# Border units in quarters, wider narrow products and filler products in a two-layer decode kernel

## The chip, the core and the metric

The kernel runs on one core of a Trainium2 chip. The metric is the device time of one execution in microseconds. A profile of one execution gives a span, from the first to the last instruction, and the times of every instruction and DMA packet.

## The reference

One token for each of 4 sequences passes twice through a grouped-query attention block over a cache and a gated feed-forward block (FFN). Both layers use the same weights and the same cache.

```python
B, Sq, D = 4, 1, 512
Hq, Hkv, Sk, Dh = 32, 8, 8192, 128          # k_cache, v_cache: [B, Hkv, Sk, Dh], bf16
F = 1792                                    # w_gate, w_up: [D, F]; w_down: [F, D]

def _A_ref(x, k_cache, v_cache, wq, wo):
    q = (x @ wq) as [B, Hq, 1, Dh]
    scores = einsum("bhqd,bhkd->bhqk", q, repeat(k_cache, 4)) * Dh ** -0.5
    o = einsum("bhqk,bhkd->bhqd", softmax(scores), repeat(v_cache, 4))
    return o as [B, 1, Hq * Dh] @ wo

def _B_ref(x, w_gate, w_up, w_down):
    return (silu(x @ w_gate) * (x @ w_up)) @ w_down

x = x + _A_ref(_layernorm(x), ...); x = x + _B_ref(_layernorm(x), ...)
x = x + _A_ref(_layernorm(x), ...); x = x + _B_ref(_layernorm(x), ...)
```

## The kernel before

**Units and slots.** A unit is one pair of sequence and key-value head: 32 in a layer, each with 2 MB of K and 2 MB of V. "K0" or "V31" below is the K or V of unit 0 or 31. SBUF holds 8 slots of 2 MB (`kvf`, seen as `kv`); slot and place in it are named `s{slot}.{block}`, 8 blocks a slot. Layer 0 goes through units 0 to 31; layer 1 (`unit_order[1]`) through 29, 30, 31, which are kept in SBUF from layer 0, and then 0 to 28. The FFN weights lie in slots 6 and 7 (gate first, then a quarter of up, then down) and in some room of their own (the rest of up), which is loaded once.

**One unit.** `keys` (lines 527 to 549) turns each block of K in place on VectorE (`turn`, a stream transpose of 128x512 words) and emits, a few blocks behind (`drain`, `LAG`), the score products of a block on TensorE (`scores`: four matmuls that stream 256 columns). After the eighth block come the softmax steps (`max_p`, `max_t`, `exps`, `turn_p`, `total`) on DVE, PE and ACT, spread over the following blocks by gaps in `line`. `values` multiplies by V: two blocks of 8 matmuls of 512 columns, then `own_first`, `own_others`, `add_rows`; the last two units of a layer take `block_last` instead, 64 matmuls of 4 columns each. After the four units of a head `out_proj` adds its share of `wo` to `xT`. `work` (line 312) sets the order: K of a unit, then V of the unit before it. The blocks that K30 and K31 of layer 1 bring have no transposes, since they were turned in layer 0.

**Loads.** All loads are issued on SP's queue in the order of the list `items`. `pump` (line 373) issues the next item when its slot (`home`) is free; a slot comes free when its unit is `finished`. SP waits, in order, on the semaphore of the engine that reads the slot. A whole unit is one DMA whose source is cut into contiguous runs (`runs`); the last V of a layer (`split`) comes in four column ranges. At the start of layer 1, V0 takes the slot of K29 and K2 that of K30, in two halves each (`half`, `halves`): the first after four blocks are scored, the second after eight. K0 and K1 go to slots 6 and 7, which `ffn` frees at its end (line 731) for the waits of the single loads.

**The border.** After the last unit `center` computes the mean and the squares, `ffn` (line 699) multiplies by gate (56 tiles of 128x128, 4 columns), up (56) and down in three groups of 6, 6 and 2 of its 14 tile rows (`WD`), with the loads of down in the same groups; `add_to_x` adds each group's product. Then layer 1 begins with `center`, the query products of unit 29's head and their rows (`qproj`), and the units. The other heads' query products (112 matmuls of 4 columns) are one entry of `blocks` before K0 (line 807).

**Emission.** PE, DVE and ACT instructions are recorded on tapes (`T.pe`, `T.op`; helper lines 99 and 117 are what the profile names) and played at the end by `roll`, which puts the longest run of alike units of each layer in a loop on each engine.

Of the kernel before, what the change touches and what calls it, by code (L numbers as in the profile page):

```python
# [145 lines left out]
def bass_interleave_layers__gqa_block_cached__swiglu_ffn__decode_kernel(  # L146
# [18 lines left out]
    P = 128  # L165
# [19 lines left out]
    RUN = 1 << 15  # L185
    assert TB == 2 * NA and NV * REP <= QB
# [4 lines left out]
    with ExitStack() as es:  # L191
# [16 lines left out]
        wd_sb = kvf[:, f1:f1 + FO * D].rearrange("p (f n) -> p f n", f=FO)  # L208
        places = [f"s{s}.{q}" for s in range(NKEEP, NSLOT) for q in range(NB)]
        room = lambda a, b: places[(a - f0) // (TB * Dh):(b - 1 - f0) // (TB * Dh) + 1]  # L210
        at_w = {"wg": room(f0, f0 + KT * F) + ["wg"], "wu": room(f0 + KT * F, f1) + ["wu", "wu3"],
                "wd": room(f1, f1 + FO * D)}
        WD = ((0, 6), (6, 12), (12, 14))
# [43 lines left out]

        SBK = [0, 1]
# [8 lines left out]
        sem_h = [[sem(f"sem_h{k}{i}") for i in range(2)] for k in range(2)]  # L267
# [57 lines left out]
        for n, it in ((3, ("wo", 0)), (6, ("wo", 1)), (9, ("wo", 2)), (12, ("wo", 3))):  # L325
            items.insert(n, it)
        ends = [i for i, it in enumerate(items) if it[0] == "wd"]
        split = {items[e - 3] for e in ends}

        halves = {("K", 1, unit_order[1][k]): items[ends[0] + 3 + k] for k in range(2)}  # L330
# [42 lines left out]
        def pump():  # L373
            while issued[0] < len(items):
                n = issued[0]
                it = items[n]
                if it[0][0] == "w":
                    if it[0] == "wg":
                        if not {NKEEP, NKEEP + 1} <= free:
                            return  # L380
                        free.difference_update((NKEEP, NKEEP + 1))
                    load_weight(*it)
                    issued[0] += 1
                    continue

                s = home(it)
                if s not in free:
                    return
                free.remove(s)
                kind, L, u = it  # L390
                slot_of[it] = s
                g, b = unit_gb(u)
                cache = A_k_cache if kind == "K" else A_v_cache
                src = cache[b, g, :, :].rearrange("(p t) d -> p (t d)", p=P)
                if it in split:
                    w = TT * Dh // NQ
                    n8 = NB // NQ
                    for q in range(NQ):
                        T.dma("sp", [(kv[:, s, q * w:(q + 1) * w], src[:, q * w:(q + 1) * w])], sem_l[q],
                              writes=[f"s{s}.{q * n8 + k}" for k in range(n8)])  # L400
                else:
                    T.dma("sp", [(kv[:, s, :], runs(cache[b, g, :, :]))], sem_s[s], writes=[f"s{s}.{q}" for q in range(NB)])
                issued[0] += 1

        def half(it, i):
            to = halves[it]
            kind, L, u = to
            s = slot_of[it]
            if i == 0:
                assert items[issued[0]] == to  # L410
                slot_of[to] = s
                issued[0] += 1
            w = SL // 2
            src = (A_k_cache if kind == "K" else A_v_cache)[u % B, u // B, :, :].rearrange("(p t) d -> p (t d)", p=P)
            T.dma("sp", [(kv[:, s, i * w:(i + 1) * w], src[:, i * w:(i + 1) * w])], sem_h[unit_order[1].index(it[2])][i],
                  writes=[f"s{s}.{i * NB // 2 + k}" for k in range(NB // 2)])

        def finished(it):
# [5 lines left out]
            elif it in halves:  # L424
                half(it, 1)
                pump()
            else:
                free.add(slot_of[it])
                pump()
# [97 lines left out]
        def keys(L, u):  # L527
            def block(q):
# [9 lines left out]
                if q == NB // 2 - 1 and ("K", L, u) in halves:  # L538
                    half(("K", L, u), 0)
# [4 lines left out]

            for q in range(NB):
                if (L, u, q) not in turned:
                    turn(L, u, q)
                blocks.append((0.65, lambda q=q: block(q)))
                drain(LAG)
        done = set()  # L550
        def values(L, u):
# [36 lines left out]
            def add_rows():  # L588
                T.pe(bank(LNB)[:, 0:REP], acc[:], head[:], reads=["acc", "head"], writes=[f"pb{LNB}"],
                     start=True, stop=True)  # L590
                scale_o(LNB)

            def block_last(q):
# [6 lines left out]
                for t in range(q * TB, (q + 1) * TB):  # L600
                    c0 = (t % TB) * QB + REP * q
                    T.pe(bank(bk)[:, 0:REP], kv[:, s, t * Dh:(t + 1) * Dh], pT[:, turn_of[u], c0:c0 + REP],
# [5 lines left out]
            def scale_o(k):  # L608
                T.op("dve", lambda e: e.tensor_tensor(oT[:, g // (G - 1), :, b], bank(k)[:, 0:REP], rl[:, rl_of[u], :],
# [21 lines left out]
        def out_proj(g):  # L631
# [10 lines left out]
            for nt in range(KT):  # L642
                for c in range(REP):
                    T.pe(bank(OUTB)[:, nt * B:(nt + 1) * B], ((c, nt), wo_at(c * D + nt * P)), o4[:, c, :], at=g,
# [7 lines left out]
        def center():  # L652
            T.op("dve", lambda e: e.tensor_reduce(vs[:], xT[:].rearrange("p (k b) -> p b k", b=B), AX.X, ALU.add),
                 reads=["x"], writes=["vs"])
            T.pe(bank(LNB)[:, 0:B], ones, vs[:], start=True, stop=True,
                 reads=["vs", "onesf"], writes=[f"pb{LNB}"])
            total = bank(LNB)[:, 0:B].unsqueeze(1).to_broadcast([P, KT, B])
# [18 lines left out]
        def qproj(gs, u=None):  # L676
            h0, nh = gs[0] * REP, len(gs) * REP
            for h in range(h0, h0 + nh):
                for kt in range(KT):
                    T.pe(bank(LNB)[:, h * B:(h + 1) * B], wq_sb[:, kt, h * Dh:(h + 1) * Dh], xn[:, kt * B:(kt + 1) * B],  # L680
                         start=(kt == 0), stop=(kt == KT - 1),
                         reads=[f"wq{kt}", "xn"], writes=[f"pb{LNB}"], sig=(kt == KT - 1))
            T.op("dve", lambda e: e.tensor_copy(qT[:, :, h0:h0 + nh],
# [5 lines left out]
            for c in range(4):  # L689
                for a in range(NA):  # L690
                    T.pe(ob[a * QB:(a + 1) * QB, c, :, h0:h0 + nh], pick[:, c // 2, :, c % 2], qT[:, :, h0:h0 + nh],
                         start=True, stop=True,
                         reads=["pT1", "ident"], writes=[f"pb{OUTB}"], sig=(a == NA - 1))
            if u is not None:
# [4 lines left out]
        def ffn(last):  # L699
# [4 lines left out]
            rb = rstd[:].unsqueeze(1).to_broadcast([P, FO, B])  # L704
            for (w_sb, wname, bk) in (([wg_sb[:, k, :] for k in range(KT)], "wg", gb), (wu_sb, "wu", ub)):
                for fo in range(FO):
# [3 lines left out]
                    for kt in range(KT):  # L710
                        T.pe(bank(bk)[:, fo * B:(fo + 1) * B], w_sb[kt][:, f:f + 2 * P - 1:2], xn[:, kt * B:(kt + 1) * B],
                             start=(kt == 0), stop=(kt == KT - 1),
                             reads=at_w[wname] + ["xn"], writes=[f"pb{bk}"], sig=(fo == FO - 1 and kt == KT - 1))
            T.op("dve", lambda e: e.tensor_tensor(fb(gr), fb(gT), rb, ALU.mult),
# [8 lines left out]
            for j, (a, b) in enumerate(WD):  # L723
                for nt in range(KT):
                    for fo in range(a, b):
                        T.pe(bank(dn[j])[:, nt * B:(nt + 1) * B], wd_sb[:, fo, nt * P:(nt + 1) * P],
                             hT[:, fo * B:(fo + 1) * B], start=(fo == a), stop=(fo == b - 1),
                             reads=["hT", f"wd{j}"] + at_w["wd"], writes=[f"pb{dn[j]}"], sig=(fo == b - 1))
                if j < len(WD) - 1:
                    add_to_x(dn[j])  # L730
            free.update((NKEEP, NKEEP + 1))
            pump()
# [65 lines left out]
        for L in range(2):  # L798
            turn_of.update((u, i % 2) for i, u in enumerate(unit_order[L]))
            rl_of.update((u, i % CYCLE) for i, u in enumerate(unit_order[L]))  # L800
            center()
            first = unit_order[L][0] // B
            qproj([first], unit_order[L][0])
            rest_q = [list(range(0, first)), list(range(first + 1, G))]
            assert (L, first) in ((0, 0), (1, G - 1))
            for i, (kind, _, u) in enumerate(work(L)):
                if L == 1 and (kind, u) == ("K", 0):
                    blocks.append((3.5, lambda gs=rest_q[0]: qproj(gs)))
                (keys if kind == "K" else values)(L, u)
                if L == 0 and i == 0:  # L810
                    drain(0.0)
                    qproj(rest_q[1])
# [45 lines left out]
```

## Time and profile before

| | |
|---|---|
| runs | 650.14 us median of 3 (649.64 to 650.25) |
| profiled execution | 651.29 us, its span 649.3 us |
| mean granted TensorE clock | 0.855 |
| PE, PEld, DVE, ACT, POOL busy | 505.3, 324.7, 446.2, 116.3, 19.3 us |
| HBM read | 273.88 MB, 422 GB/s over the span |
| whole-unit loads, issue to landing | 28.8 us (K), 31.2 us (V) |
| score matmuls, 128x256 | x2048, 332.6 us busy, 305 ns mean |
| DVE transposes of K, 128x512 | x488, 322.3 us busy, 686 ns mean |

PE is TensorE's matmul row, PEld its weight loads, SPq SyncE's issue of DMAs. A line such as `ps<-kvf,zq 128*128 128x256 bf16` is a matmul into PSUM with a stationary tile of 128x128 and 256 streamed columns. Busy times of PE are of pipelined matmuls, so they overlap. Times in timelines count from the start of the span.

### The profile page before, as it was taken

The page shows a single profiled execution, that of the slowest core. Times are in us where ns is not written, and L with a number is a line of the kernel's source. Part 1 is how long each engine was busy: PE and PEld are TensorE (multiplying, and loading weights), DVE is VectorE, ACT ScalarE, POOL GpSimd, SP SyncE. Part 2 cuts the span into 40 slices and gives each one's busy share as a digit, 9 for nine tenths or more (in the row PEclk, how much of TensorE's full clock was granted, in tenths as well). Part 3 has the DMA queues.
Part 4 walks back from the last instruction along what each step waited for, and adds up shares of the span by engine and source line. Part 5 has one row for each costly group of instructions (what it writes and reads, how often), then busy time and mean ns, then how long its engine had stood idle before and what let it go on. Part 6 is the DMA issues. An engine that isn't in the chain of part 4 may idle for free.

```text
span 649.3 us, 12407 instructions
## 1 busy us (share of the span) xinstructions
PE 505.3 (78%) x4896; PEld 324.7 (50%) x4896; DVE 446.2 (69%) x1079; ACT 116.3 (18%) x391; POOL 19.3 (3%) x73
## 2 busy tenths in 40 slices
PE   1657788878868787886877986898888787886886
PEld 1534454545435454553556654555555454553556
DVE  2556676776866767776762386979797777686683
ACT  0021111211211212221220211213131221121120
POOL 0000000000000000000000000000000000000000
PEclk9998787797987879789795978979897969799795
DMA  8999999999999999999999999999999999999996
GB/s 347 427 431 428 433 429 434 428 440 428 432 436 424 444 426 432 439 424 442 428 416 361 421 408 430 417 439 430 432 438 424 438 430 436 436 424 438 430 415 279
DMA packets 13085, 274.27 MB, mean 422 GB/s; under 512 B 2712, under 2 KB 2720, under 8 KB 3744
## 3 DMA queue, kind: packets, MB, share of 16 engines
q1 hardware_dynamic: 13056, 273.89, 98.7%
q8 instruction: 17, 0.28, 0.2%
q14 instruction: 12, 0.10, 0.0%
HBM read 273.88 MB, written 0.00 MB: 422 GB/s over the span
## 4 chain that ended last, share of the span: by engine, by line
DMA 50%; DVE 24%; PE 21%; issue 3%; SPq 1%; ACT 1%; DVEq 0%; POOL 0%; ACTq 0%; POOLq 0%
DMA kvf<-in_A_k_cache_dram 47%; PE ps L99 21%; DVE kvf L117 15%; DVE acc L117 4%; DMA kvf<-in_B_w_up_dram 3%; DVE one L117 1%; DVE pT L117 1%; SPq L135 1%; DVE m L117 1%; DVE scr L117 1%; ACT pb L117 0%; ACT acc L117 0%; DVE oT L117 0%; DVEq L782 0%; SPq L133 0%
## 5 line engine op out<-in xcount | busy, mean ns | idle before, releaser
L117 DVE STREAM_TRANSPOSE kvf<-kvf 128x512 f32<-128x512 f32 x488 | 322.3, 686 | 68.6 <-DMA kvf<-in_A_k_cache_dram 68.6
L99 PE MATMUL ps<-kvf,zq 128*128 128x256 bf16 x2048 | 332.6, 305 | 21.7 <-DVE kvf L117 16.4
L99 PEld LDWEIGHTS ps<-kvf,zq 128*128 128x128 bf16 x2048 | 202.6, 111 | 92.7 <-DVE kvf L117 40.2
L117 ACT ACTIVATE pb<-m 1x128 f32<-1x128 f32 x64 | 19.7, 308 | 441.1 <-DVE m L117 441.1
L99 PE MATMUL ps<-kvf,pT 128*16 128x512 bf16 x960 | 68.0, 407 | 1.4 <-DVE rl L117 1.4
L117 DVE SCALAR_TENSOR_TENSOR acc<-ps,own,acc 128x128 f32<-128x128 f32 x180 | 63.2, 351 | 6.5 <-ACT acc L117 1.9
L99 PE MATMUL ps<-identf,one 128*1 128x128 f32 x64 | 17.9, 279 | 43.2 <-DVE one L117 43.2
L117 DVE TENSOR_REDUCE one<-ps 128x1 f32<-128x256 f32 x64 | 25.9, 405 | 37.0 <-PE ps L99 36.5
L99 PEld LDWEIGHTS ps<-identf,one 128*1 128x1 f32 x64 | 5.1, 80 | 73.6 <-DVE one L117 67.5
L99 PE MATMUL ps<-head,acc 128*128 128x4 f32 x120 | 24.5, 275 | 21.4 <-DVE acc L117 21.3
L99 PEld LDWEIGHTS ps<-head,acc 128*128 128x128 f32 x120 | 20.5, 214 | 37.0 <-DVE acc L117 36.7
L117 ACT ACTIVATE pb<-ps,one,rstd 128x256 bf16<-128x256 f32 x64 | 36.1, 563 | 2.1
L467 POOL TENSOR_TENSOR zq<-scr,quad 128x64 bf16<-128x64 bf16 x62 | 18.1, 293 | 604.0 <-PE ps L99 564.9
L99 PEld LDWEIGHTS ps<-kvf,pT 128*16 128x16 bf16 x960 | 19.1, 91 | 33.8 <-issue 21.9
L99 PE MATMUL ps<-one,pb 1*128 1x1 f32 x128 | 26.2, 272 | 11.5 <-ACT pb L117 11.2
L99 PEld LDWEIGHTS ps<-one,pb 1*128 1x128 f32 x128 | 20.8, 202 | 28.8 <-ACT pb L117 26.0
L99 PE MATMUL ps<-o,wo_sb 128*128 128x4 bf16 x256 | 26.5, 166 | 9.1 <-DVE o L117 9.1
L117 DVE STREAM_TRANSPOSE pT<-pb 128x256 bf16<-128x256 bf16 x64 | 26.1, 408 | 9.7 <-ACT pb L117 9.7
L99 PEld LDWEIGHTS ps<-rsm,one 128*128 128x128 f32 x128 | 23.9, 232 | 12.2 <-ACT rsm L117 10.4
L99 PEld LDWEIGHTS ps<-o,wo_sb 128*128 (+1 forms) x256 | 22.8, 103 | 12.8 <-issue 9.0
L99 PE MATMUL ps<-rsm,one 128*128 128x4 f32 x128 | 21.7, 240 | 9.0 <-ACT rsm L117 9.0
L117 DVE TENSOR_TENSOR xT<-xT,ps 128x16 f32<-128x16 f32 x21 | 3.6, 172 | 33.1 <-PE ps L99 33.1
(61 smaller groups left out, 197.1 us busy)
## 6 DMA issues: line engine op xcount, KB each, us to landing
kvf<-in_A_k_cache_dram SPq DMA_DIRECT2D x60, 2048.0 KB, 28.8
kvf<-in_A_v_cache_dram SPq DMA_DIRECT2D x58, 2048.0 KB, 31.2
wq_sb<-in_A_wq_dram SPq DMA_DIRECT2D x4, 1024.0 KB, 8.4
wo_sb<-in_A_wo_dram SPq DMA_DIRECT2D x8, 512.0 KB, 37.7
kvf<-in_A_v_cache_dram SPq DMA_DIRECT2D x8, 512.0 KB, 14.7
kvf<-in_B_w_gate_dram SPq DMA_DIRECT2D x8, 448.0 KB, 16.8
kvf<-in_B_w_down_dram SPq DMA_DIRECT2D x14, 256.0 KB, 17.6
kvf<-in_B_w_up_dram SPq DMA_DIRECT2D x5, 448.0 KB, 18.0
```

The lines of the kernel that those rows point to most:

```text
L99: return e.matmul(out, lhsT=lhsT if at is None else lhsT(place(at)), rhs=rhs, **kw)
L117: self.tape[engname].append((repr((name, args, kw)), lambda e, _: getattr(e, name)(*args, **kw), left, sig, None))
L135: ins = e.add_instruction(mybir.InstDMACopy(name=self.nc.get_next_instruction_name(), mode="Copy", queue="qSPDynamicHW", ins=e.lower_ap_dm ...
L467: T.op(eng, lambda e: e.tensor_tensor(dst, q4, m4_, ALU.mult), reads=keys_ + ["quad"], writes=["zq"])
```

## The change

It has four parts. (1) The units at the borders (the last of each layer, and 0, 1 and 2 of layer 1, `fours`) are laid out as four contiguous quarters of their tokens and loaded by quarters (`part`); V0 and K2 come into the slots of K29 and K30 by quarters, after every second scored block (`quarter`, `heirs`); K0 and K1 are issued inside `ffn`, piece by piece: three quarters of K0 after the gate products, the fourth after up, half of K1 after the first group of down, half after the last. The groups of down are 8, 4 and 2, and each names its own places. (2) The order at the start of layer 1: K0 and K1 are turned while K30 and K31 are scored (`ahead`); V31 comes before K0; V3 is loaded before K4; the query products of the other heads become seven entries and their rows an eighth. (3) Products of 4 columns repeat them to 32 (`few`, `WIDE`); the 28 others overwrite columns of the bank that are not yet, or no longer, in use. (4) `warm` adds products that nobody reads to the start of layer 1: two and one around the sum in `center`, one after the first query products, one after their rows. `qproj` is split into `qmul` and `qrows` for it, and `add_rows` moves to other columns of its bank.

```diff
+    WIDE = 32
...
-        WD = ((0, 6), (6, 12), (12, 14))
+        WD = ((0, 8), (8, 12), (12, 14))
...
-                "wd": room(f1, f1 + FO * D)}
+                **{f"wd{j}": room(f1 + a * D, f1 + b * D) + [f"wd{j}"] for j, (a, b) in enumerate(WD)}}
...
+        def few(ap):
+            n = ap.shape[1]
+            return ap.unsqueeze(1).to_broadcast([P, WIDE // n, n])
...
+        i, j = (items.index((k, 1, unit_order[1][2 * NRES + n])) for k, n in (("K", 1), ("V", 0)))
+        items[i], items[j] = items[j], items[i]
...
+        heirs = {("K", 1, unit_order[1][k]): items[ends[0] + 3 + k] for k in range(2)}
+        fours = {(L, unit_order[L][-1]) for L in range(2)} | {(1, u) for u in unit_order[1][NRES:2 * NRES]}
...
+        def part(it, s, a, b, sem_):
+            kind, L, u = it
+            n = NB // NQ
+            w, m = n * TB * Dh, S // NQ
+            src = (A_k_cache if kind == "K" else A_v_cache)[u % B, u // B, :, :]
+            T.dma("sp", [(kv[:, s, q * w:(q + 1) * w], runs(src[q * m:(q + 1) * m, :])) for q in range(a // n, b // n)],
+                  sem_, writes=[f"s{s}.{k}" for k in range(a, b)])
...
+        def quarter(it, i):
+            to = heirs[it]
+            if i == 0:
+                place(to, slot_of[it])
+            n = NB // NQ
+            part(to, slot_of[it], i * n, (i + 1) * n, sem_h[unit_order[1].index(it[2])][i])
...
-                if q == NB // 2 - 1 and ("K", L, u) in halves:
-                    half(("K", L, u), 0)
+                if ("K", L, u) in heirs and (q + 1) % (NB // NQ) == 0 and q < NB - 1:
+                    quarter(("K", L, u), q // (NB // NQ))
...
+            i = unit_order[L].index(u)
+            ahead = unit_order[1][i + 2] if L == 1 and i in (1, 2) else u
             for q in range(NB):
-                if (L, u, q) not in turned:
-                    turn(L, u, q)
+                if (L, ahead, q) not in turned:
+                    turn(L, ahead, q)
...
-                    T.pe(bank(bk)[:, 0:REP], kv[:, s, t * Dh:(t + 1) * Dh], pT[:, turn_of[u], c0:c0 + REP],
+                    T.pe(bank(bk)[:, 0:WIDE], kv[:, s, t * Dh:(t + 1) * Dh], few(pT[:, turn_of[u], c0:c0 + REP]),
...
+        def warm(n=1):
+            for _ in range(n):
+                T.pe(bank(SBK[1])[:, 0:SW], wq_sb[:, 0, 0:P], wq_sb[:, 0, 0:SW], reads=["wq0"], writes=[f"pb{SBK[1]}"],
+                     start=True, stop=True)
...
-        def center():
+        def center(n=0):
...
+            warm(2 * n)
             T.pe(bank(LNB)[:, 0:B], ones, vs[:], start=True, stop=True,
                  reads=["vs", "onesf"], writes=[f"pb{LNB}"])
+            warm(n)
...
+            ks = items[ends[0] + 1:ends[0] + 3]
+            w6 = KT * F // (TB * Dh) // 2 * 2
...
+                if not last:
+                    if bk == gb:
+                        place(ks[0], NKEEP)
+                        part(ks[0], NKEEP, 0, w6, sem_p[0])
+                    else:
+                        part(ks[0], NKEEP, w6, NB, sem_p[1])
...
+                if j == 0 and not last:
+                    place(ks[1], NKEEP + 1)
+                    part(ks[1], NKEEP + 1, 0, NB // 2, sem_p[2])
-            free.update((NKEEP, NKEEP + 1))
-            pump()
+            if not last:
+                part(ks[1], NKEEP + 1, NB // 2, NB, sem_p[3])
...
-            center()
+            center(L)
...
+            todo = work(L)
+            if L == 1:
+                todo.remove(("V", 1, unit_order[1][2]))
+                todo.insert(todo.index(("K", 1, 0)), ("V", 1, unit_order[1][2]))
...
-                if L == 1 and (kind, u) == ("K", 0):
-                    blocks.append((3.5, lambda gs=rest_q[0]: qproj(gs)))
+                if L == 1 and (kind, u) == ("V", unit_order[1][2]):
+                    for k in rest_q[0]:
+                        blocks.append((0.5, lambda k=k: qmul([k])))
+                    blocks.append((0.5, lambda gs=rest_q[0]: qrows(gs)))
```

## The prediction

> **What bounds the kernel.** I read the page's queue table and chain of waits first, then a table of windows, then SP's and PE's timelines around the places that the windows pointed to.
>
> ```profile
> q1 hardware_dynamic: 13056, 273.89, 98.7%
> ...
> DMA 50%; DVE 24%; PE 21%; issue 3%; SPq 1%; ACT 1%; DVEq 0%; POOL 0%; ACTq 0%; POOLq 0%
> ```
>
> The reader is to see that one queue moves 273.89 MB and is nearly always occupied, and that half of the chain is DMA. So the time is bytes over rate, plus the stretches in which the stream does not run at its rate. The windows (start:end, length, busy time and count of PE, PEld, DVE, ACT, POOL, then granted clock, DMA share, GB/s) give both:
>
> ```profile
> 100.00:300.00 200.00, 159.91 (x1294) 98.19 (x1291) 144.18 (x338) 35.91 (x122) 6.15 (x21) 0.84 1.00 433
> ...
> 325.00:345.00 20.00, 15.38 (x298) 12.10 (x299) 11.64 (x36) 4.10 (x14) 0.29 (x1) 0.83 0.99 415
> 345.00:350.00 5.00, 3.19 (x108) 2.93 (x105) 0.85 (x6) 0.00 (x0) 0.00 (x0) 0.50 0.94 303
> 350.00:355.00 5.00, 3.55 (x45) 2.82 (x46) 1.47 (x9) 0.56 (x2) 0.00 (x0) 0.50 0.75 321
> 355.00:360.00 5.00, 4.50 (x26) 2.95 (x24) 0.42 (x1) 0.00 (x0) 0.29 (x1) 0.64 0.99 421
> 360.00:380.00 20.00, 18.18 (x256) 13.37 (x257) 9.44 (x26) 5.07 (x17) 0.58 (x2) 0.89 1.04 442
> 380.00:385.00 5.00, 5.00 (x42) 3.15 (x43) 3.72 (x8) 0.00 (x0) 0.29 (x1) 0.75 0.96 377
> 385.00:390.00 5.00, 4.04 (x33) 2.65 (x31) 4.92 (x14) 1.77 (x6) 0.00 (x0) 1.00 0.92 374
> 390.00:400.00 10.00, 5.23 (x47) 3.10 (x48) 6.53 (x15) 1.77 (x6) 0.29 (x1) 0.98 0.98 419
> 400.00:420.00 20.00, 17.96 (x155) 10.85 (x155) 17.91 (x42) 4.42 (x16) 0.88 (x3) 0.92 1.01 428
> ...
> 645.00:649.30 4.30, 1.66 (x36) 1.22 (x36) 0.87 (x4) 0.00 (x0) 0.00 (x0) 0.50 0.00 1
> ```
>
> In the steady stretch the stream moves 433 GB/s. At that rate 273.89 MB take 632.5 us, so 16.8 us of the 649.3 us span are lost somewhere. A window's loss is its length times (1 - GB/s / 433). The border between the two layers loses 1.50, 1.29, 0.14, -0.42, 0.65, 0.68, 0.32 and 0.23 us from 345 to 420: together **4.4 us**. The rows for 300 to 325 and for 420 to 625 stand at 430 to 433. The last 4.3 us carry nothing. What may be won lies in these two places.
>
> SP's timeline says why the border loses:
>
> ```profile
> 347.99 2.38 SPq L135 DMA_DIRECT2D kvf<-in_A_k_cache_dram  x2
> 356.84 3.07 SPq L133 DMA_DIRECT2D kvf<-in_A_v_cache_dram  x2
> 362.13 2.85 SPq L133 DMA_DIRECT2D kvf<-in_A_k_cache_dram  x2
> 365.63 0.48 SPq L135 DMA_DIRECT2D kvf<-in_A_v_cache_dram  x1
> 370.70 0.48 SPq L135 DMA_DIRECT2D kvf<-in_A_k_cache_dram  x1
> 371.69 0.47 SPq L135 DMA_DIRECT2D kvf<-in_A_v_cache_dram  x1
> 383.63 0.47 SPq L135 DMA_DIRECT2D kvf<-in_A_k_cache_dram  x1
> ```
>
> The first load after the FFN weights (K of unit 0, "K0") goes out at 347.99, when the up products are done; K1 needs the down products (350.4). In 345 to 350 the stream moves 303 x 5 = 1.5 MB, 3.5 us' worth, so the weights run out near 348.5. A new transfer needs one to two microseconds before it flows (the output store, 4 KB, takes from 647.79 to about 649.1). Nothing is queued behind the weights: that is the hole. The second hole follows the issue at 383.63: K4, which waits until K0 is scored.
>
> **The change, part by part.** (1) *Rooms given up in pieces.* Gate products end at 343.8 (DVE reads their bank then). From there SP issues three quarters of K0; after up (347.9) the fourth; after the first down group one half of K1; after the last the other half. A unit is 2.097 MB, 4.84 us at 433 GB/s, a quarter 1.21 us. Supply then runs: weights to 348.5, three quarters to 352.1, the fourth (issued 348) to 353.3, K1's halves (issued about 349.3 and 350) to 355.8 and 358.2. Each is issued at least 4 us before its turn, against the 2 us that I allow. Hole one closes: 1.50 + 1.29 + 0.14 = 2.9 us.
>
> (2) *V0 and K2 in quarters* into the slots of K29 and K30. They must be issued by 356.2, 357.4, 358.7, 359.9 (V0) and 361.1 to 364.7 (K2). K29 is scored from 352.93 to 359.5, so its quarters fall at about 354.6, 356.2, 357.9, 359.5: in time. K30 is scored from 359.99 to 364.57: 361.1, 362.3, 363.4, 364.6, in time with nothing to spare. V1 must go by 365.9 (it went at 365.63), K3 by 370.8 (370.70), V2 by 375.6 (371.69).
>
> (3) *Turning K0 and K1 ahead.* Sixteen DVE transposes of about 0.65 us, 10.4 us, move from after 376 to the scoring of K29 to K31. DVE has room: from 345 to 380 it is busy 12.2 of 35 us. But they sit in DVE's queue among the softmax steps of units 29 to 31, which TensorE, the V products, and so SP's loads wait for. Cost: none if they fill only idle time; if each unit takes the 7.05 us of the steady loop (max steps at 410.86 and 417.90 on PE) in place of 5.1 and 6.1 us here (DVE reductions at 359.54, 364.61, 370.66), K30 is up to 2.0 us late and K31 up to 2.9, and the stream loses as much. I take 0.7 us of loss over (2) and (3) together, since three of the transposes lie before K29's maximum, where DVE idles 6.5 us.
>
> (4) *V31 and its slot first; V3 loaded ahead of K4; query products by groups.* V3 needs V31's slot, and V31 now precedes K0. It must go by 380.5, K4 by 385.3. The 112 query products (2.94 us) and their copies move with their old length; with K30 and K31 at 7 us, V31 ends near 377.5, and K0, already turned, is scored near 381.5. Both in time: the second hole (0.65 + 0.68 us) and most of the trickle to 420 (0.55) close. All holes closed are 4.4 us, less the 0.7 of (3): **-3.7 us**. Bounds: -4.4, and -1.5 with 2.9 lost in (3).
>
> (5) *Products of four columns stream 32.* 1104 products (256 V, 256 wo, 256 q, 224 gate and up, 112 down). The trace has none of 32 columns; bounds come from its neighbours:
>
> ```profile
> 348.22 1.65 PE L99 MATMUL ps<-scr,kvf 128*128 128x4 bf16 x56 [0.31 <-DVE scr L117]
> ...
> 613.46 1.05 PE L99 MATMUL ps<-kvf,zq 128*128 128x256 bf16 x8
> ...
> 627.39 1.51 PE L99 MATMUL ps<-kvf,zq 128*128 128x256 bf16 x12
> ```
>
> Four columns cost 1.65 / 56 = 29 ns each at clock 0.50, and 1.75 us for 64, 27 ns, around 337 at a higher clock: not streaming, which would halve, but a floor. At clock 1.00, 256 columns cost (1.51 - 1.05) / 4 = 115 ns, 0.45 ns a column with the weight load hidden. So 32 columns stream 14 ns, 29 ns at clock 0.50: under the floor, or just at it. Low end 0; high end, if the 28 extra columns came on top, 13 ns at 1.00 and 25 ns at 0.50. I take 0, as weight loads do hide behind 256 columns. The Trainium skill ("TensorE: Matmul & The Clock Gate", section "Wait — 56ns, not 53.3ns?") gives about 25 ns from start to start for 32 columns at full clock, by which this term would be nothing too.
>
> (6) *Fillers.* Five 256-column products in the border, about 0.21 us each at clock 0.50, in waits of 0.27 to 0.68 us that PE has there on DVE. Hidden; uncovered they push K29 by under 0.5 us, and its quarters have up to 1.6 us in hand. If they and (5) lift the clock (0.50 from 345 to 355), K29's scoring shortens by up to 3 us, which only adds cover. I count no gain.
>
> (7) *Down groups 8, 4, 2.* At the end, after 645.69, PE still has 21 products (0.70 us) though the last weights have landed; with a second group of 16 in place of 24 it should have about 8, 0.25 us: -0.4 us. Bounds: 0 and -0.9 (with a higher clock for the transposes).
>
> (8) *Quarters as contiguous runs; more issues.* SP issues 22 more loads at 0.42 us; it idles for hundreds of microseconds in waits, and a quarter streams 1.21 us. Queued behind each is only the next load. Nothing. The two V splits lose their 4 KB pieces, units 0 to 2 gain pieces of 16 KB: nothing, bounds -0.4 and +1.5 (12.6 MB at the 411 to 415 GB/s of the windows with small pieces).
>
> **Sum.** -3.7 - 0.4 = -4.1 us. The profiled execution took 651.29 us (span 649.3); it should become 647.2 (span 645.2). The runs' median is 1.15 us below the profiled time, 650.14, and becomes **646.0 us**. Its own range is 644.4 to 647.5.
>
> **Rivals.** (A) *Late hand-over*: the transposes delay K30, V29 and K31 as in (3); the hole moves to 361 to 372 and costs 2.0 to 2.9 us, say 2.7, in place of 0.7. For it: K30's quarters have no slack. Against: DVE idles 6.5 us before. Time: 648.0.
>
> (B) *Given back at the loop's entry*: ACT stands 5.4 us with nothing to wait for while K2 is scored, and PE with it (idle 4.2 us to 399.75). K6's load was issued at 403.0; a stream 3.7 us earlier wants it near 400. If the stall stays in its place the gain goes back there: about 650. Against: K0 and K1 already turned bring K2 forward some 4 us.
>
> (C) *Slower: 32 columns on top of the weight load.* The place is the last FFN at clock 0.50: 40 V products after the last quarter lands, 16 wo, 112 gate and up, 56 down, 224 x 25 ns = 5.6 us on the closing path, no DMA to hide them. 650.14 - 3.7 + 5.6 = 652.0. It decides from 18 ns a product. Against: the floor argument in (5).
>
> (D) *Small loads stream slowly.* From the windows, 12.6 MB at 411 GB/s cost 1.5 us: 647.5. The Trainium skill ("DMA: Bandwidth & Descriptors", section "Measured (HBM→SBUF, 128 partitions, SWDGE, issued from GpSimd)") advises at least 1 MiB a transfer and gives 341 GB/s there; by it, an estimate, the six units would lose 7.8 us and the kernel end near 654. The window 360 to 380, which holds 1 MB halves queued behind each other, runs at 442.
>
> (E) *It does not do what it says*: the clock stays 0.50 over the border. That costs nothing in my sum.
>
> **Chances.** Forecast 0.56, (A) 0.18, (B) 0.09, (C) 0.11, (D) 0.06 (half of it slower than before). A measurement here tells about 0.2%, 1.3 us, from no change: faster needs under 648.8. Faster is the forecast, most of (A), half of (D) and a little: 0.77; same 0.10; slower 0.13. The range for 8 in 10 runs from 644.4 to 649.3: the forecast's and (A)'s.
>
> **What would show it.** SP's loads of K0 near 344 instead of 348; the windows from 345 to 355 above 415 GB/s; K4's window near 433; 56 down products still in about 1.65 us; V0's and K2's quarters at the times above. Wrong if the windows 360 to 375 fall to about 350 (A), 395 to 405 (B), or if the last FFN takes over 2 us longer (C).

## The result and the profile after

Over 20 runs of each kernel on one chip the changed kernel takes 648.83 us (median; 647.65 to 650.71) and the kernel before 650.25 us (649.10 to 652.38): a ratio of 0.9977, 95% interval 0.9971 to 0.9983. It is **1.4 us faster**, where 4.1 us were forecast. The profiled execution took 648.43 us, its span 646.5 us, mean granted clock 0.858.

The page's queue row and chain of waits look as before; the stream is still the bound:

```profile
q1 hardware_dynamic: 12768, 273.90, 99.0%
...
DMA 52%; DVE 22%; PE 19%; issue 3%; SPq 2%; ACT 1%; DVEq 0%; POOL 0%; ACTq 0%; POOLq 0%
```

The windows of the changed kernel over the border (start:end, length, busy time and count of PE, PEld, DVE, ACT, POOL, granted clock, DMA share, GB/s):

```profile
345.00:350.00 5.00, 3.86 (x85) 2.83 (x81) 1.07 (x7) 0.00 (x0) 0.00 (x0) 0.50 1.04 429
350.00:355.00 5.00, 4.74 (x52) 3.23 (x52) 2.88 (x10) 0.56 (x2) 0.00 (x0) 0.50 1.02 429
355.00:360.00 5.00, 4.50 (x32) 3.25 (x31) 1.80 (x4) 0.00 (x0) 0.29 (x1) 0.79 1.00 383
360.00:365.00 5.00, 5.00 (x52) 3.33 (x49) 4.72 (x12) 1.52 (x5) 0.29 (x1) 1.00 0.97 360
365.00:370.00 5.00, 4.35 (x45) 3.05 (x46) 4.92 (x13) 1.77 (x6) 0.00 (x0) 1.00 0.98 400
370.00:380.00 10.00, 9.05 (x179) 6.19 (x172) 4.14 (x13) 2.14 (x7) 0.29 (x1) 0.83 1.02 434
380.00:385.00 5.00, 4.50 (x40) 3.50 (x37) 1.49 (x4) 0.31 (x1) 0.29 (x1) 1.00 1.05 446
385.00:390.00 5.00, 4.82 (x48) 3.03 (x48) 3.24 (x8) 1.77 (x6) 0.29 (x1) 1.00 0.97 419
390.00:420.00 30.00, 22.61 (x193) 13.47 (x193) 24.16 (x57) 6.53 (x22) 0.88 (x3) 0.89 1.01 428
```

With the prediction's formula, length times (1 - GB/s / 433), the rows lose 0.05, 0.05, 0.58, 0.84, 0.38, -0.02, -0.15, 0.16 and 0.35 us: **2.2 us, against 4.4 before**. Both holes of before are closed: 345 to 355 went from 303 and 321 GB/s to 429, 380 to 390 from 377 and 374 to 446 and 419. A **new hole** of 1.8 us stands from 355 to 370, where the kernel before lost nothing. Its DMA share stays at 0.97 to 1.00 while the rate falls to 360: the engines show no idle time, their packets take longer. A packet of 16 KB normally takes 0.61 us; here single engines show up to 1.9 us.

SP's timeline of the changed kernel shows that this is not late issuing by the prediction's own due times:

```profile
342.70 7.73 SPq L135 DMA_DIRECT2D kvf<-in_A_k_cache_dram  x8
353.96 4.73 SPq L135 DMA_DIRECT2D kvf<-in_A_v_cache_dram  x4
359.76 3.99 SPq L135 DMA_DIRECT2D kvf<-in_A_k_cache_dram  x4
364.27 2.39 SPq L135 DMA_DIRECT2D kvf<-in_A_v_cache_dram  x4
369.68 0.47 SPq L135 DMA_DIRECT2D kvf<-in_A_k_cache_dram  x1
370.66 1.74 SPq L135 DMA_DIRECT2D kvf<-in_A_v_cache_dram  x3
```

The rows are K0 and K1 (eight quarters), V0, K2 (four each), V1, K3 and the first three quarters of V2. Inside the merged rows V0's quarters go out at 353.96, 355.66, 357.33 and 358.21, K2's at 359.76, 360.76, 362.06 and 363.28: all 1.3 to 2.2 us ahead of the times that step (2) demanded. On time, and still the stream thinned.

PE's timeline of the changed kernel, for later use the up products of the first FFN and the first 28 score products of K29, then the end:

```profile
343.97 1.65 PE L99 MATMUL ps<-xn,kvf 128*128 128x32 bf16 x56 [1.35 <-DMA kvf<-in_B_w_up_dram]
...
352.86 5.27 PE L99 MATMUL ps<-kvf,zq 128*128 128x256 bf16 x28
...
641.02 1.06 PE L99 MATMUL ps<-scr,kvf 128*128 128x32 bf16 x35 [0.44 <-DVE scr L117]
642.86 0.68 PE L99 MATMUL ps<-scr,kvf 128*128 128x32 bf16 x21 [0.77 <-issue]
643.87 0.59 PE L99 MATMUL ps<-identf,xn 128*4 128x128 bf16 x4 [0.34 <-DVE xn L117]
```

The end has 35 down products, a stop of 0.77 us for which the profile names no releaser ("issue"), then 21, as before the change (0.32 us there).

So the two profiled spans, 649.3 and 646.5 us, differ by 2.2 us at the border and some 1.0 us at the start, less 0.2 us that the end got longer: 3.0 us where 2.8 are to be explained, as near as these sums come. The start varies by itself: in the first 25 us the changed kernel lost 2.2 us in this execution and 3.2 in a second one; the kernel before lost 3.2.

### The profile page after: what moved, and what is told of

Read it like the earlier page. It is cut to its first block, busy times and chain, and to the rows that moved or that the text cites. A ratio compares the mean times of both kernels' runs of the same rounds, so it can differ in the third digit from the quotient of the medians.

```text
span 646.5 us, 12450 instructions
## 1 busy us (share of the span) xinstructions
PE 508.0 (79%) x4901; PEld 327.0 (51%) x4901; DVE 446.8 (69%) x1079; ACT 116.6 (18%) x391; POOL 19.3 (3%) x73
## 4 chain that ended last, share of the span: by engine, by line
DMA 52%; DVE 22%; PE 19%; issue 3%; SPq 2%; ACT 1%; DVEq 0%; POOL 0%; ACTq 0%; POOLq 0%
DMA kvf<-in_A_k_cache_dram 47%; PE ps L99 19%; DVE kvf L117 14%; DVE acc L117 4%; DMA kvf<-in_B_w_gate_dram 3%; DMA kvf<-in_B_w_down_dram 2%; SPq L135 2%; DVE pT L117 1%; DVE one L117 1%; DVE m L117 1%; DVE scr L117 0%; DVEq L823 0%; DVE oT L117 0%; ACT pb L117 0%; ACT acc L117 0%
## 5 line engine op out<-in xcount | busy, mean ns | idle before, releaser
L99 PE MATMUL ps<-o,wo_sb 128*128 128x32 bf16 x256 | 26.7, 183 | 9.3 <-DVE o L117 9.3
```

The source lines that it names most:

```text
L99: return e.matmul(out, lhsT=lhsT if at is None else lhsT(place(at)), rhs=rhs, **kw)
```

## The experiments

The changed kernel was run a second time, and nine edits of it, one of them twice, each beside the kernel before on one chip. Two figures come from each trace by the same formula: the loss of the new hole (355 to 370) and of the whole border (345 to 420). "Clock back" is when the granted clock returned to 1.00, which the windows give as well: 355 + 5 x (1 - 0.79) / 0.50 = 357.1 in the table above.

| kernel | clock back | 355-370 | 345-420 | median us | ratio to before |
|---|---|---|---|---|---|
| before | 358.6 | 0.0 | 4.4 | | 1 |
| changed | 357.1 | 1.8 | 2.2 | 648.83 | 0.9977 [0.9971, 0.9983] |
| changed, again | 357.8 | 2.0 | 2.7 | 649.25 | 0.9982 [0.9973, 0.9991] |
| 4 columns, no fillers | 356.4 | 1.3 | 1.7 | 649.04 | 0.9972 [0.9963, 0.9982] |
| K0, K1 late | 355.4 | 0.3 | 2.7 | 650.54 | 0.9991 [0.9982, 1.0001] |
| quarters in pairs (issue times as changed, see there) | 358.2 | 2.3 | 3.3 | 648.83 | 0.9964 [0.9950, 0.9978] |
| old order | 357.1 | 1.8 | 3.1 | 649.28 | 0.9973 [0.9963, 0.9984] |
| more fillers | 351.6 | 0.3 | 1.2 | 648.23 | 0.9963 [0.9950, 0.9976] |
| more fillers, again | 356.2 | 1.6 | 2.0 | 648.55 | 0.9964 [0.9952, 0.9977] |
| more fillers, 4 columns | 357.4 | 2.3 | 3.3 | 649.16 | 0.9975 [0.9961, 0.9989] |
| 16 products at the start | 353.5 | 0.5 | 0.7 | 647.94 (one run) | |
| 16 products before the last FFN | 356.0 | 1.8 | 2.4 | 648.79 (one run) | |
| 28 products before the last FFN | 356.1 | 1.6 | 2.2 | 650.24 (one run) | |

The losses are of one profiled execution each, the times are medians of 5 to 20 runs except for the last three rows. The kernels ran in batches, each beside the kernel before (650.25, 651.20, 650.63 and 650.69 us), so kernels of different batches are compared by their ratios. A border loss varies by half a microsecond or more between executions of one kernel, so the two columns can be compared only roughly.

### The issue of K0 and K1, alone

K0 and K1 go out at the end of the FFN again; all else stays.

```diff
-                    if bk == gb:
-                        place(ks[0], NKEEP)
-                        part(ks[0], NKEEP, 0, w6, sem_p[0])
-                    else:
-                        part(ks[0], NKEEP, w6, NB, sem_p[1])
+                    pass
...
-                if j == 0 and not last:
-                    place(ks[1], NKEEP + 1)
-                    part(ks[1], NKEEP + 1, 0, NB // 2, sem_p[2])
             if not last:
-                part(ks[1], NKEEP + 1, NB // 2, NB, sem_p[3])
+                place(ks[0], NKEEP); part(ks[0], NKEEP, 0, NB, sem_p[0])
+                place(ks[1], NKEEP + 1); part(ks[1], NKEEP + 1, 0, NB, sem_p[1])
```

> The changed kernel, but K0 and K1 are issued where the kernel before issued them (after the up products and after the last down products). Theory: the hole from 345 to 355 opens again, 2.5 to 2.9 us, while the later hole (355 to 370, 1.7 us) closes, because V0's and K2's quarters then have more lead: net 0.9 to 1.6 us slower than the changed kernel, 649.7 to 650.4. Rival: the early issue carries the whole border gain and the later hole has another cause: 2.0 us or more slower, 650.8 or above.

Measured: 650.54 us, ratio 0.9991 [0.9982, 1.0001], by the ratios 0.6 to 0.9 us slower than the changed kernel, at or just under the low end of what was expected; the interval touches those of the changed kernel. Its windows:

```profile
345.00:350.00 5.00, 3.43 (x102) 2.92 (x98) 0.55 (x3) 0.00 (x0) 0.00 (x0) 0.50 0.85 328
350.00:355.00 5.00, 4.62 (x50) 2.89 (x49) 1.49 (x9) 0.56 (x2) 0.00 (x0) 0.50 1.01 344
355.00:360.00 5.00, 4.50 (x39) 3.56 (x38) 3.83 (x8) 0.00 (x0) 0.29 (x1) 0.96 1.00 419
360.00:365.00 5.00, 5.00 (x51) 3.21 (x48) 4.72 (x11) 1.58 (x6) 0.29 (x1) 1.00 1.01 426
```

The first hole is back (2.2 us in 345 to 355) and the second is gone (0.3 us in 355 to 370). The stream, held up earlier, asks for V0 and K2 later, and the same handing over of slots is then in time: V0's fourth quarter goes out at 358.08 and K2's first at 359.63, in the changed kernel at 358.21 and 359.76, so it is the demand that moved and not the issue. The two holes are one budget: closing the first (2.1 us of difference up to 355) opens 1.5 us of the second.

### The products of 32 columns and the fillers, alone

```diff
-    WIDE = 32
+    WIDE = 4
...
-            for _ in range(n):
+            for _ in range(0):
```

> The changed kernel with products of 4 columns again and without the five fillers; everything else stays. Theory: the products cost 27 to 29 ns either way and the granted clock is 0.50 for 20.5 us around the border in both traces, so these two parts do nothing: 648.8 us, within 0.4. Rival: the wider products and fillers are what carries part of the gain (the clock stands at 1.00 for 3.4 us in the last FFN of the changed kernel): 649.5 or more.

Measured: 649.04 us, ratio 0.9972 [0.9963, 0.9982], the same as the whole change. Parts (3) and (4) of the change bring nothing and cost nothing that these runs can tell. PE's timeline of this kernel has the 56 up products as

```profile
344.79 1.66 PE L99 MATMUL ps<-xn,kvf 128*128 128x4 bf16 x56 [2.30 <-DMA kvf<-in_B_w_up_dram]
```

1.66 us with 4 columns, and 1.65 with 32 in the line of the changed kernel above: 29 to 30 ns each at clock 0.50. The Trainium skill ("TensorE: Matmul & The Clock Gate", section "Wait — 56ns, not 53.3ns?") gives a floor of about 25 ns from start to start. The trace agrees that there is a floor, and puts it at 29 to 30 ns where each product brings its own weights, at clock 0.50; the section's example of 32 columns is at the full clock.

### The order of the work, undone

No turning ahead, V31 after K0, K4 before V3, the query products in one piece, as in the kernel before.

```diff
-        items[i], items[j] = items[j], items[i]
+        pass
...
-            ahead = unit_order[1][i + 2] if L == 1 and i in (1, 2) else u
+            ahead = u
...
-                todo.remove(("V", 1, unit_order[1][2]))
-                todo.insert(todo.index(("K", 1, 0)), ("V", 1, unit_order[1][2]))
+                pass
```

> The changed kernel with the order of before: K0 and K1 turned at their own place, V31 after K0, K4 loaded ahead of V3, the query products in one piece. Theory: the hole at 380 to 390 opens again and is larger than before the change (1.3 us), since the stream is 2 us earlier: 2 to 3 us slower, 650.8 to 651.8. Rival: K30's and K31's quarters come sooner without the transposes in DVE's queue, which gives back 0.7 us or more: at most 1 us slower, below 649.8.

Measured: 649.28 us, ratio 0.9973 [0.9963, 0.9984]: no difference from the change that these runs can tell, where 2 to 3 us were expected. In its windows the second hole of the kernel before is back:

```profile
360.00:365.00 5.00, 5.00 (x51) 3.34 (x49) 1.61 (x5) 1.53 (x6) 0.29 (x1) 1.00 0.94 344
...
380.00:385.00 5.00, 4.82 (x43) 2.84 (x41) 4.28 (x10) 1.02 (x4) 0.29 (x1) 0.90 1.01 354
385.00:390.00 5.00, 4.21 (x42) 2.42 (x41) 4.92 (x13) 0.75 (x3) 0.29 (x1) 1.00 0.98 419
```

380 to 390 lose 1.1 us where the changed kernel loses nothing, and the whole border 3.1 against 2.2. That microsecond isn't seen in the medians, whose intervals are as wide; what becomes of it is open. The first row settles another point: without a single transpose moved ahead (DVE busy 1.61 of 5 us against 4.72), the window 360 to 365 is as thin as with them. Rival (A)'s mechanism, transposes that delay units 29 to 31, is not the cause.

### V0 and K2 in pairs of quarters

The program now asks for two quarters after the fourth scored block and for two after the eighth; that was meant to send every other quarter later.

```diff
-                if ("K", L, u) in heirs and (q + 1) % (NB // NQ) == 0 and q < NB - 1:
-                    quarter(("K", L, u), q // (NB // NQ))
+                if ("K", L, u) in heirs and q == NB // 2 - 1:
+                    quarter(("K", L, u), 0); quarter(("K", L, u), 1)
...
+                quarter(it, NQ - 2)
                 quarter(it, NQ - 1)
```

> The changed kernel with the same eight 512 KB loads of V0 and K2, but issued two at a time after the fourth and the eighth scored block. Theory (the hole from 355 to 370 is a late hand-over: the 16 DMA engines run up to 3.4 us apart and the early ones run dry): every other quarter comes 1.0 to 1.7 us later, the hole grows by 0.8 to 1.5 us, 649.6 to 650.3. Rival (the pieces of 16 KB stream slowly): the pieces are the same, so 648.8 within 0.4.

Measured: 648.83 us, ratio 0.9964 [0.9950, 0.9978], not slower than the change, against the expectation. SP's timeline says why the expectation had nothing to stand on:

```profile
355.72 4.40 SPq L135 DMA_DIRECT2D kvf<-in_A_v_cache_dram  x4
361.20 3.99 SPq L135 DMA_DIRECT2D kvf<-in_A_k_cache_dram  x4
```

Inside the first row the quarters go out one by one, at 355.72, 357.43, 358.76 and 359.65, and the first of them 2.21 us after K29's first score product (353.51), exactly as in the changed kernel (351.75 and 353.96). K2's four take the same 3.99 us. The edit moves the loads within SP's program, but each load still waits for the readers of its own two blocks alone (`part` names them), and so it starts when it started before. This run is therefore the changed kernel once more, and it tests neither theory nor rival. That pieces of 16 KB stream slowly is answered elsewhere: the same pieces lose 0.3 us with K0 and K1 late. What the run does show is how far two batches of one and the same schedule differ: 0.9964 here, 0.9977 and 0.9982 in the other two. Its trace has the hole of the changed kernel:

```profile
355.00:360.00 5.00, 4.57 (x28) 3.13 (x25) 1.44 (x4) 0.37 (x2) 0.28 (x1) 0.68 0.96 354
360.00:365.00 5.00, 4.93 (x45) 3.64 (x49) 4.69 (x11) 1.52 (x5) 0.22 (x2) 1.00 0.98 344
365.00:370.00 5.00, 4.34 (x44) 3.02 (x37) 4.92 (x12) 1.77 (x6) 0.08 (x1) 1.00 1.01 403
```

2.3 us are lost here against 1.8, with the clock back at 358.2, the latest of all executions but that of the kernel before.

### More fillers: the pace of unit 29

The wide products did not raise the clock. This kernel puts more unread 256-column products into PE's waits: six after gate, three after up, more around the sum in `center` and after the first query products.

```diff
                 if not last:
+                    warm(6 if bk == gb else 3)
...
-            warm(2 * n)
+            warm(3 * n)
...
-            warm(n)
+            warm(2 * n)
...
-            warm(L)
+            warm(2 * L)
```

> The changed kernel with more fillers at the border: six after gate, three after up, and five and two in place of three and two around the start of layer 1. Theory (the quarters of V0 and K2 come at the pace at which K29 is scored, at clock 0.50): with the clock at 1.00 from about 352, K29's 32 score products take 3.7 instead of 6.2 us, the quarters come 1 to 2 us sooner, the stream loses under 0.7 instead of 1.6 us from 355 to 370, and the kernel is 0.7 to 1.3 us faster than the changed one run beside it. Rival (pieces, or engines apart whatever the lead): the loss from 355 to 370 stays above 1.3 us. Should the clock stay 0.50, the run decides nothing but the price of the fillers.

> The changed kernel unchanged, beside the others on the same chip. Theory: the border loses about 3 us of stream from 335 to 430 as in the first profile, and PE stands still again at the 36th down product of the last FFN. Time 0.2% below the kernel before.

Measured in one batch: 648.23 us, ratio 0.9963 [0.9950, 0.9976], beside 649.25 us, 0.9982 [0.9973, 0.9991], for the changed kernel run again. The windows, a stop among the up products and the scoring of K29 in the kernel with more fillers, two views of one execution:

```profile
350.00:355.00 5.00, 4.76 (x72) 3.27 (x69) 3.20 (x13) 0.56 (x2) 0.00 (x0) 0.84 0.97 390
355.00:360.00 5.00, 4.50 (x40) 3.50 (x37) 2.95 (x7) 0.31 (x1) 0.29 (x1) 1.00 1.02 413
360.00:365.00 5.00, 4.83 (x48) 3.12 (x49) 4.72 (x11) 1.81 (x7) 0.29 (x1) 1.00 1.01 426
365.00:370.00 5.00, 4.52 (x56) 3.07 (x55) 4.18 (x12) 1.18 (x4) 0.00 (x0) 1.00 1.03 436
```

```profile
347.82 0.44 PE L99 MATMUL ps<-xn,kvf 128*128 128x32 bf16 x11 [1.79 <-issue]
...
353.98 3.27 PE L99 MATMUL ps<-kvf,zq 128*128 128x256 bf16 x28
```

The 28 products take 3.27 us at clock 1.00; in the changed kernel, most of the time at 0.50, they take the 5.27 us of its line above. V0's quarters go out every 0.89 us (354.66, 355.55, 356.44, 357.33) in place of 1.70, 1.67 and 0.88 us, and the new hole shrinks from 1.8 to 0.3 us. The transposes ahead are all there (DVE busy 4.72 from 360 to 365, the same as in the changed kernel), so again it isn't they. What remains of the gain is held down by a stop: PE halts 1.79 us behind the 45th up product ("issue"; the section on the halt comes back to it), K0's fourth quarter goes out at 348.29 in place of 345.66, and 350 to 355 falls to 390 GB/s, 0.5 us. By the budget above, these 0.5 us also help the quarters behind them; from 345 to 370 together the loss is 0.9 us, in the changed kernel 1.9, so about 1.0 us is left for the pace.

Is it the fillers or luck? The same kernel ran once more, and a third with the added fillers and 4 columns:

> The kernel with more border fillers once more, for its time and a second trace. Theory (late hand-over): clock 1.00 before 353, under 0.7 us of stream lost from 355 to 370, 0.3 to 0.45% below the kernel before. Rival (the first run was lucky in the phase of the clock's windows, 3.4 us long): clock back at 1.00 only near 357, loss 1.4 us or more, 0.2% below.

> The kernel with more border fillers, but products of four columns as before the change. Theory: the 256-column fillers alone bring the clock back, the wider products add nothing: clock 1.00 before 353.5 and the time of the kernel with fillers, within 0.5 us. Rival: without the wider products the windows stay too empty, the clock is back at 1.00 only near 356, and the loss from 355 to 370 is 1.3 us or more again.

Measured: 648.55 us, ratio 0.9964 [0.9952, 0.9977], and 649.16 us, 0.9975 [0.9961, 0.9989]. In the second execution of the kernel with more fillers the clock fell again just before K29:

```profile
345.00:350.00 5.00, 3.44 (x81) 2.43 (x77) 0.85 (x5) 0.00 (x0) 0.00 (x0) 0.84 1.06 436
350.00:355.00 5.00, 4.92 (x52) 3.16 (x52) 3.04 (x11) 0.56 (x2) 0.00 (x0) 0.50 0.99 419
355.00:360.00 5.00, 4.50 (x36) 3.39 (x35) 1.73 (x4) 0.00 (x0) 0.29 (x1) 0.88 1.00 370
360.00:365.00 5.00, 5.00 (x51) 3.33 (x50) 4.72 (x11) 1.52 (x5) 0.29 (x1) 1.00 0.95 360
```

It stood at 1.00 until 349.3, at 0.50 until 356.2, and the hole is back, 1.6 us. So one and the same program has the hole or not by where the clock's changes fall. The stretches at 0.50 are multiples of some 3.4 us (6.8 here, 20.5 in the changed kernel), and their phase differs from one execution to the next. The Trainium skill ("TensorE: Matmul & The Clock Gate", section "What's actually happening") describes a free-running window of 3413 ns over which TensorE's activity is judged; the traces agree in length and in the wandering phase. Over the executions of the kernels that close hole one, the new hole is 0.3 us where the clock was back at 351.6 and 1.3 to 2.3 us in the nine where it was back at 356.0 or later; what lies between is shown by one execution further down, 0.5 us at 353.5. The time of this second run, 0.9964 again, does not follow its one profiled hole.

Beside the changed kernel in one batch the median with more fillers is 1.0 us lower (0.9963 to 0.9982), though the intervals overlap by a little. Since the changed schedule reached 0.9964 too, as the run in pairs, a gain in time from the fillers is not shown. Whether the wide products help beside the added fillers (0.9964 with, 0.9975 without) can't be told from these intervals.

### The halt at the end

Behind the 35th of the last 56 down products PE waits for nothing that the profile names. In the trace a 16 KB packet of the queue called "instruction" ends 1.25 us before PE goes on (640.58 + 1.03 = 641.61, then 642.86; before the change 643.40 + 1.03 = 644.43, then 645.69); over all halts of the kept traces it is 1.2 to 1.5 us. If PE's own program arrives in such packets, the halt belongs to a place in the program's text and not to the 35th product. Three kernels move the text by unread 4-column products: 16 at the very start, ahead of both layers, or 16 and 28 between the last `center` and the last FFN. The diff is that of the second:

```diff
             center()
+            for _ in range(16 * L):
+                T.pe(bank(SBK[1])[:, 0:B], ident, ident[:, 0:B], reads=["ident"], writes=[f"pb{SBK[1]}"], start=True, stop=True)
             ffn(L == 1)
```

> The changed kernel with 16 unread four-column products at its very start, where PE waits for x. Theory (PE's halt in the last down products is a fetch of instructions): the halt moves to the 20th down product, 16 earlier, and the end does not come sooner. Rival (PE waits there for the down weights): it stays behind product 32 or 48, where the weight groups begin.

> The changed kernel with 16 unread four-column products between the last center and the last FFN, behind the last loop. Theory (the halt sits at a fixed place of PE's program, counted from the loop's end, because the next instructions have not arrived): if PE halts in the down products, it halts behind product 19 or 20 in place of 35. Rival (it sits at a fixed product, whatever comes before): behind product 35. No halt in this one execution would decide nothing.

> The same with 28 unread products. Theory: a halt behind down product 7 or 8, or none seen because PE waits there for the silu anyway. Rival: behind product 35.

Sixteen at the start (647.94 us, one run): the halt stays behind product 35. That was a miss of the theory as it was put; products ahead of the loops do not move it. By chance the clock of that execution was back at 353.5, and its new hole was 0.5 us. At the border this program is the changed one, K29's scoring begins 0.2 us sooner, and hole one is closed (0.2 us up to 355): it is the cleanest point for the pace of unit 29, 0.8 us lost from 345 to 370 where the changed kernel lost 1.9. Sixteen before the last FFN (648.79 us, one run) move it to product 19 = 35 - 16, and 28 (650.24 us, one run) to product 7 = 35 - 28, as this view of PE's timeline with 28 shows:

```profile
641.97 0.37 PE L99 MATMUL ps<-scr,kvf 128*128 128x32 bf16 x7 [0.44 <-DVE scr L117]
643.95 1.47 PE L99 MATMUL ps<-scr,kvf 128*128 128x32 bf16 x49 [1.61 <-issue]
645.75 0.59 PE L99 MATMUL ps<-identf,xn 128*4 128x128 bf16 x4 [0.33 <-DVE xn L117]
```

The border between the layers has such a halt too, and had it before the change, behind the 51st of the 56 up products; the chain of waits of the kernel before reads (start, length, what):

```profile
344.74 1.50 PE ps L99 x51
346.24 1.38 issue
```

Six further kernels or executions have it at the same product, the second execution of the changed kernel among them (1.37 us); four have none, the first one among them. With six fillers between gate and up it stands behind the 45th = 51 - 6 (1.79 and 1.38 us, more fillers with 32 and with 4 columns). So the text moves it here as well, and the stop of the kernel with more fillers is not a new one.

The place in the text is shown; that the packet brings PE's program is inferred from its queue's name and from the time between. When the packet is sent is not: in the second execution of the changed kernel (where a halt was expected), in the one with pairs and in the one with more fillers and 4 columns there was no halt at the end at all; with more fillers (first execution) and with late K0 and K1 PE waited there for the last weights instead; elsewhere the halt was 0.3 to 1.6 us. What sets that moment is open.

## Why the prediction was right in direction and wrong in size

The chain, in the prediction's steps, for the profiled executions:

- **(1) Rooms in pieces: right.** K0's first load at 342.70 (343.8 foreseen, 347.99 before); 345 to 355 at 429 GB/s. Hole one, 2.9 us, lost 0.1 us up to 355, and the kernel with K0 and K1 late has 2.2 of it back. What the step did not see is the halt of 1.38 us among the up products before: K0's issue at 347.99 waited for it too, so not all of hole one was the order of the loads.
- **(2) V0 and K2 by quarters: the step that failed.** It allowed 2 us from issue to flow and found every quarter in time. Every quarter did go out 1.3 to 2.2 us ahead of that, and the stream lost 1.8 us from 355 to 370. The term for (2) and (3), 0.7 us, measured 1.8; with 0.4 us of remains elsewhere (0.1 up to 355, 0.35 from 390 on) that is the whole shortfall of the border, 2.2 us won for 3.7. The start-up of 2 us was right: the first increment of V0's first three quarters comes 3.2 to 3.4 us after the issue, 1.2 us of them streaming. Wrong was to reckon with one stream. The 16 DMA engines of the queue are not in step, and a quarter gives each only two packets. A load raises its semaphore in 16 increments, read here as one for each engine (the trace does not name the engines); for V0's quarters and K2's first it has

```
first increment   357.13  358.99  360.74  361.99  363.82
last increment    360.52  361.75  362.96  364.18  365.52
```

The latest engine takes a quarter every 1.2 to 1.3 us, its full rate, so it never lacks work. The earliest, 3.4 us ahead of it, takes 1.86 and 1.75 us for the second and third: it waits for quarters issued 1.7 us apart, until it has lost half of its head start. By these times what is lost is lost on the early engines. In the kernel with more fillers the second to fourth quarter go out 3.0 to 4.0 us before the earliest engine has finished the one ahead, in the changed kernel 1.5 to 2.5 us. The other traces agree. Call lead the time from a quarter's issue until the earliest engine ends the load ahead of it: the smallest lead among V0's and K2's quarters is 1.5 to 1.7 us in the nine executions with a hole of 1.3 to 2.3 us, and 2.7, 2.8 and 4.1 us in the three with 0.5, 0.3 and 0.3 us. The lead has to cover the start of a transfer for the earliest engine; the due times of the prediction stood for the mean. The kernel before was spared because its halves had leads of 2.9 to 3.4 us, with the demand put off by hole one. Hole one also brought its engines nearer together, K0's increments to within 0.64 us (355.38 to 356.02); but the engines stand 2.4 us apart in the kernel with K0 and K1 late, which has no such hole either, so it is the lead that decides.
- What sets the lead is the pace at which K29 is scored, and so the clock: **(6)** and **(E)** priced a clock of 0.50 over the border at nothing, "only adds cover". It is worth about 1 us of stream: from 345 to 370 the two executions with the clock back at 351.6 and 353.5 lose 0.9 and 0.8 us, the first of the changed kernel 1.9. (E) came true, its price was wrong.
- **(3) Turning ahead: cheaper than feared.** The maxima of units 29, 30 and 31 are reduced on DVE at 358.17, 363.24 and 369.64 (before: 359.54, 364.61, 370.66); no unit is late. (A) named the right place and nearly the right size, 2.0 to 2.9 us, for the wrong reason.
- **(4) Order: right in the trace.** V3's load at 378.03 (due by 380.5) and K4's at 382.34 (385.3) are in time, and 380 to 420 lose 0.4 us where they lost 1.9. In the medians the experiment that undoes it shows no difference.
- **(5), (8), rivals (C) and (D): nothing, as taken.** 32 columns cost what 4 cost. Quarters of 512 KB queued behind each other run at 429 GB/s (345 to 355). Against this stands the advice of the Trainium skill ("DMA: Bandwidth & Descriptors", section "Measured (HBM→SBUF, 128 partitions, SWDGE, issued from GpSimd)") of at least 1 MiB a transfer: it does not bind a deep queue, and the quarters were slow only where each was issued just ahead of its turn.
- **(7) Down groups: nothing for -0.4.** I read the 21 products after the last weights as lateness of the weights. They stand behind the halt in PE's program, which stayed (0.77 us for 0.32). From the landing of the last weights to the end it takes 4.1 us, 3.85 before.
- **(B)** did not happen: 390 to 420 runs at 428, before at 425.

The border's gain in the trace is 2.2 us in one execution and 1.7 in the other, the runs' 1.4. The rest would lie in the kernel before, of which one profile exists; it isn't traced further. Of the 2.7 us that the forecast had too much, 1.5 are thus the border in the first execution, 0.6 the end (0.2 longer for 0.4 shorter), and the cause of the rest is open.

## What to carry to other kernels

A hole that is closed moves every later demand of the stream forward by as much; ask at once which hand-over is then late, and by the pace of which engine at which clock. A load that is issued just in time needs a lead of its start-up reckoned to the earliest of the DMA engines, which can be 3 us ahead of the latest; here 1.7 us were too few and 2.7 enough. Small pieces should need it more than large ones, since an engine has only a packet or two of each, though no run here compares them. A halt that no semaphore explains, at the same instruction in every run, may be the program's own text arriving: move the text and see whether the halt moves.

## What was not expected of the hardware

- The engines of one DMA queue stand some 2.2 us apart in the steady stream of 433 GB/s, up to 3.1 us at the border while it still moves 429 GB/s, and a hole brings them nearer together (0.64 us). When they run dry one by one, the DMA share stays near 1.00 and only GB/s falls.
- PE's halt at a place of its program's text, 0.3 to 1.8 us, which ends 1.2 to 1.5 us after a packet of the instruction queue; there is one in each FFN, and products added ahead of it in the same stretch move it by as many products.
- The granted clock's stretches of some 3.4 us have another phase in each execution, and so one program has or hasn't a hole: 1.6 us in one execution, 0.3 in another.
